# T5-bias attention and a maxout FFN in one kernel: transposes of q, k and x by DMA, and by TensorE

## The chip, the cores and the metric
The kernel runs on one core of one Trainium2 chip. The metric is device time in microseconds, the median of several runs.

## What is computed
Attention over 8 batches, 8 heads, 576 positions and 64 channels a head, with a T5 bias that depends on |i - j| alone, and after it an FFN that takes the largest of three products:

```python
scores = scale * np.matmul(q, k.transpose(0, 1, 3, 2))
scores = scores + bias.transpose(2, 0, 1)[None, :, :, :]   # bias_table[bucket(|i - j|)]
attn = np.exp(scores - scores.max(-1, keepdims=True)); attn = attn / attn.sum(-1, keepdims=True)
x = np.matmul(attn, v).transpose(0, 2, 1, 3).reshape(B * S, H * D)      # 4608 x 512
h = np.maximum(np.maximum(x @ w1, x @ w2), x @ w3)                      # 4608 x 768
out = h @ w_out                                                         # 4608 x 512
```
Inputs and output are float32; the kernel's matmuls work in bfloat16.

## The kernel before
**Visits.** The unit of work is a visit: one batch and one pair of heads, written (b, hp), 32 in all. Batch 0 has a prologue of its own (lines 1098 to 1195); batches 1 to 7 run through the main loop at line 1211. The 576 positions are four tiles of 128 and a rest of 64 (the tails, qtail and ktail, in which the rests of two heads stand on a diagonal). The 128 partitions of a pair hold 64 channels of one head and 64 of the other, so q and k are needed turned, channels on the partitions: qT[128, hp, 576] and kT[128, hp, 640].

**A visit.** TensorE makes scores into a score tile (pool ps_s, tag "sc": two tiles of two PSUM banks each, used in a ring also by the left keys, the left queries and batch 1's transposes). ScalarE takes the exponential into e4 (`scores` line 843, `key_scores` 854), VectorE multiplies the band near the diagonal by the exponential of the bias (`times_band` 803, `times_bandt` 906, `times_band_left` 918). One visit later `attend` (926) or `attend_rows` (976) multiplies by v, with a column of ones for the sums, and VectorE divides into x_sb (`quotients`). x_sb has positions on the partitions; the FFN wants xT, channels on the partitions.

**FFN.** It runs in chunks of 512 tokens beside the attention: chunk b-1 is spread over the visits (b, 2) to (b+1, 1), and what is left follows after the last visit. `ffn` (393) makes the parts: gates (two of the six blocks of 128 rows at a time, three products each, the largest of them), and outputs. `fill` (709) puts queued parts at given places of the plain visits; the tiled visits have them written out in a fixed order.

**Two forms of a tiled visit.** Before ROWS = (3, 0) a tiled visit uses `plain_gates` (492) and `attend` with single banks. From ROWS on ("rows") PSUM is shared out anew (`free_banks`, `banks(1)`, line 1220), all matmuls have 64 rows and run in pairs, one on each half of the array (`pair` 370, `gates` 518, `attend_rows`), and the third product of a visit's gates is made in the next visit (`thirds`). The order of one such visit is in `run` (557): FFN rows, the maximum of the visit before, `more_scores` (the fourth key score), bands, FFN rows, left queries, `ahead` (the first key score of the next visit), FFN rows.

**Transposes.** Batch 0's q, k and x are turned on TensorE into FFN banks (`first_transposes`, `more_transposes`, `x_transposes`). Batch 1's q and k are turned on TensorE into a score tile by `second_transposes` (781): all ten transposes, then VectorE copies q, ScalarE copies k. For batches 2 to 7 `transposes` (724) turns q and k by DMA transposes on SP's queue, ten a batch, at places listed in `places` (1198); x of batches 1 to 7 goes by DMA transposes at the end of the last quotients of a batch (969 and 1017).

**Order.** `inorder` keeps the order of the program on each engine, and all matmuls, transposes and copies named here are in order. The framework orders accesses to one PSUM tile by different engines; `other_banks` (128) lifts that between copies that read different banks. Loads stand on POOL's queue; `begin_qk` (206) begins the loads of a batch two ahead.

Of the kernel before, what the change touches and what calls it, by code (L numbers as in the profile page):

```python
# [39 lines left out]
def kernel(  # L40
# [12 lines left out]
    nc = tc.nc  # L53
# [3 lines left out]
    P = 128  # L57
# [3 lines left out]
    QS = 2 * P  # L61
    QM = 2 * QS
    KT = 4
    ROWS = (3, 0)
    DEEP = 6
    PACKETS = 6 * QM
    FCH = d_ff // P
# [32 lines left out]
    def free_banks():  # L100
        ps_f.release()
        ps_a.release()
# [9 lines left out]
    def tr(*args):  # L112
        inorder(nc.tensor.transpose(*args))
# [14 lines left out]
    def other_banks(later, earlier):  # L128

        for a in later:  # L130
            for b in earlier:
                tc.declare_no_dep(a.ins, b.ins, reason="they read different PSUM banks")
# [588 lines left out]
            hook()  # L721


    def transposes(b):

        made = qk_tiles()
        qk.append(made)

        def pair(g):
            for j in range(2):  # L730
                inorder(nc.sync.dma_start_transpose(  # L731
                    out=made[j][:, g, 0 : KT * P].rearrange("p (t n) -> p t n", t=KT),
                    in_=batch[b][j][:, g].rearrange("p t h d -> p (t h d)"),
                ))

        def left():
            for j, n in enumerate((S - KT * P, P)):
                inorder(nc.sync.dma_start_transpose(  # L738
                    out=made[j][:, :, KT * P : KT * P + n],
                    in_=(qtail, ktail)[j][b % 2][0:n].rearrange("p h c -> p (h c)"),  # L740
                ))

        return [lambda: pair(0), left] + [lambda g=g: pair(g) for g in range(1, HP)]

    def qk_tiles():
        return [qkt.tile([P, HP, n], BF16, tag=x, name=x) for x, n in (("qT", S), ("kT", (KT + 1) * P))]

# [30 lines left out]
        tr(tp[:, QS : QS + P], qtail[0][:, hp, :], ident[:])  # L778
        dve_copy(qk[0][0][:, hp, QS:], tp[:, 0 : S - QS])

    def second_transposes(made, hp):

        hs = slice(2 * hp, 2 * hp + 2)
        tp = ps_s.tile([P, 2, 2 * CH], BF16, tag="sc", name="tp")
        for j, tl in enumerate((qtail, ktail)):
            for t in range(KT):
                tr(tp[:, j, P * t : P * t + P], batch[1][j][:, t, hs, :].rearrange("p h d -> p (h d)"), ident[:])
            tr(tp[:, j, KT * P : KT * P + P], tl[1][:, hp, :], ident[:])
        main = [
            copy(  # L790
                made[j][:, hp, 0 : KT * P].rearrange("c (p t) -> c p t", t=KT),
                tp[:, j, 0 : KT * P].rearrange("c (t p) -> c p t", t=KT),
            )
            for j, copy in enumerate((dve_copy, act_copy))
        ]
        tail = [
            copy(made[j][:, hp, KT * P :], tp[:, j, KT * P : n])
            for j, (copy, n) in enumerate(((dve_copy, S), (act_copy, (KT + 1) * P)))
        ]
        other_banks([main[1], tail[1]], [main[0], tail[0]])  # L800
        other_banks([tail[0]], [main[1]])

    def times_band(hp, e4, t, lo, hi, put=lambda x: x):
        lo, hi = max(lo, P * t - P), min(hi, P * t + 2 * P)
# [121 lines left out]
    def attend(b, hp, e4, el, half):  # L926

        x = ps_a.tile([P, 6, AW], F32, tag="a", name="a")
        v, vl = vx[b % 2], vt[b % 2]
        for i in range(2):
            t = 2 * half + i
            c = slice(P * t, P * t + P)
            mm(
                x[:, 2 * i : 2 * i + 2, :], lhsT=el[:, c], rhs=vl[:, hp, :, 0:AW],
                start=True, stop=False, skip_group_check=True,
            )
            for par in range(2):  # L940
                for kt in range(KT):
                    mm(
                        x[:, 2 * i + par, :], lhsT=e4[:, kt, par, c], rhs=v[:, kt, 2 * hp + par, 0:AW],
                        start=False, stop=(kt == KT - 1), skip_group_check=True,
                    )
        n = 2 + half
        if half:
            mm(
                x[:, 4:6, :], lhsT=el[:, S - P : S], rhs=vl[:, hp, :, 0:AW],
                start=True, stop=False, skip_group_check=True,  # L950
            )
            for par in range(2):
                for kt in range(KT):
                    mm(
                        x[:, 4 + par, :], lhsT=el[:, S - 64 + P * kt + 64 * par :][:, 0:P],
                        rhs=v[:, kt, 2 * hp + par, 0:AW],
                        start=False, stop=(kt == KT - 1), skip_group_check=True,
                    )

        def quotients():  # L960
            rd = nrm.tile([P, 6], F32, tag="rd", name="rd")
            inorder(nc.vector.reciprocal(rd[:, 0 : 2 * n], x[:, 0 : 2 * n, D]))
            divided[b, hp, half] = inorder(nc.vector.tensor_tensor(
                out=x_sb[b][:, 2 * half : 2 * half + n, P * hp : P * hp + P].rearrange("p t (h d) -> p t h d", d=D),
                in0=x[:, 0 : 2 * n, 0:D].rearrange("p (t h) d -> p t h d", h=2),
                in1=rd[:, 0 : 2 * n].rearrange("p (t h) -> p t h", h=2).unsqueeze(3).to_broadcast([P, n, 2, D]),
                op=ALU.mult,
            ))
            if b and hp == HP - 1:
                for t in range(2 * half, 2 * half + 2 + half):  # L970
                    c = b * S + P * t
                    w = min(P, S - P * t)
                    inorder(nc.sync.dma_start_transpose(out=xT[:, :, c : c + w], in_=x_sb[b][P - w :, t, :]))
        return quotients

    def attend_rows(b, hp, e4, el):
# [28 lines left out]
        def end():  # L1005
            behind_rows(rows(True)[0], last)

            def quotients():
                n = KT + 1
                rd = nrm.tile([P, 2, n], F32, tag="rd", name="rd")  # L1010
                a = x[:, :, 0 : n * AW].rearrange("p h (t d) -> p h t d", d=AW)
                inorder(nc.vector.reciprocal(rd[:], a[:, :, :, D]))
                inorder(nc.vector.tensor_tensor(
                    out=x_sb[b][:, 0:n, P * hp : P * hp + P].rearrange("p t (h d) -> p h t d", d=D),
                    in0=a[:, :, :, 0:D], in1=rd[:].unsqueeze(3).to_broadcast([P, 2, n, D]), op=ALU.mult,
                ))
                if hp == HP - 1:
                    for t in range(n):
                        c = b * S + P * t
                        w = min(P, S - P * t)  # L1020
                        inorder(nc.sync.dma_start_transpose(out=xT[:, :, c : c + w], in_=x_sb[b][P - w :, t, :]))
            return quotients
        return end

# [107 lines left out]
    for hp in range(HP):  # L1132
# [42 lines left out]
        else:  # L1175
# [11 lines left out]
            if hp == 2:  # L1187
                x_transposes(2, 0)
                x_transposes(3, 0)
            else:  # L1190
                begin_qk(2)
                x_transposes(0, 1)
                fill(8, lambda: second_transposes(qk[1], 0))
            products(hp, el)
        late.append(lambda hp=hp, e4=e4, el=el: attend(0, hp, e4, el, 1))

    turns = {n: [] for n in range(2, B)}
    places = {2: ((1, 1, 0), (1, 1, 1), (1, 2, 0), (1, 3, 1), (2, 1, 0)), 3: ((2, 2, 0), (2, 2, 1), (2, 3, 0), (3, 0, 0), (3, 0, 1))}
    for n in range(4, B):
        places[n] = tuple((n - 1, hp, half) for hp, half in ((1, 0), (1, 1), (2, 0), (2, 1), (3, 0)))  # L1200

    def turn_ahead(*place):

        for n, order in places.items():
            if place == order[0]:
                turns[n] = transposes(n)
            if place in order:
                turns[n].pop(0)()

    turned = [lambda hp=hp: x_transposes(hp, 1) for hp in range(1, HP)]  # L1210
    for b, hp in [(b, hp) for b in range(1, B) for hp in range(HP)]:
# [5 lines left out]
        tiled = bool(stages)  # L1217
        rows = (b, hp) >= ROWS
        if (b, hp) == ROWS:
            free_banks()  # L1220
            ps_a, ps_f = banks(1)
            pending.clear()
            thirds = [after]
        rate = 8 if b == 1 or (b, hp) == (2, 0) else 13


# [13 lines left out]
            for c, tt in order[:2]:  # L1240
                scores(qT, kT, e4, c, tt)
        store_outputs()
        turn_ahead(b, hp, 0)
        early()
        if turned:
            turned.pop(0)()
# [19 lines left out]
        if rows:  # L1266
# [19 lines left out]
            def ahead():  # L1286
# [3 lines left out]
                    key_scores(*(x[:, n % HP, :] for x in qk[n // HP]), begun[0][0], 0)  # L1290

            run(
                lambda: key_scores(qT, kT, e4, 3), left, ahead, largest, bands, lambda: left_keys_rows(qT, kT, el)
            )
            thirds.append(after)
        elif tiled:
# [35 lines left out]

            visit(qT, kT, e4, order[2:], None if together else beside_scores, el=el if together else None)
        store_outputs()
        turn_ahead(b, hp, 1)
        early()
        if turned:
            turned.pop(0)()
        if not together:
            quotients = next_late()  # L1340
            times_band(hp, e4, 1, 0, QM, inorder)
            quotients()
        if b == 1 and hp + 1 < HP:
            second_transposes(qk[1], hp + 1)
        if hp == 1 and b > 1:
            pending.extend((n, [fn]) for n, fn in rest)
            rest.clear()
# [1 line left out]
        if hp == 1 and b + 1 < B:  # L1349
# [7 lines left out]
            if b == 1:  # L1357
                load_last_weights()
            load_pair(b + 1, 3)
        if hp == (2 if b == 1 else 1) and b + 2 < B:  # L1360
            begin_qk(b + 2)

        def queries():
# [24 lines left out]
    store_outputs()  # L1388
    for put in [next_late() for _ in late[:]]:
        put()  # L1390
    fill(13)
    store_outputs()
    for n in range(B - 1, NCH):
# [37 lines left out]
```

## Time and profile before
| | |
|---|---|
| median of 3 runs | 307.38 us (306.70 to 309.17) |
| the profiled execution | 306.96 us, its span 305.2 us |
| granted TensorE clock | 1.000 |
| ScalarE exponentials e<-sc, 128x1024 | 128 of 1026 ns |
| FFN matmuls psp<-xT,w_bf, 64x512 | 784 of 376 ns (latency of one; they overlap) |
| software queue q0 (loads) | 105664 packets, 95.5% of 16 engines' span |
| hardware queue q1 (stores and transposes) | 58304 packets, 41.6% |
| DMA transposes xT<-x_sb | 35, 5.6 us from issue to landing |
| DMA transposes qT<-q_sb and kT<-k_sb | 24 and 24, 5.8 and 5.6 us |
| DMA transposes of the tails | 6 and 6, 6.3 and 6.8 us |

The span is the time from the first to the last instruction of the core in one profiled execution; the execution's time has a little more around it. The share of busy time is a mean over stages with different limits, so stages are read by windows. A matmul's duration is its latency: matmuls follow each other faster than that, so the distance between starts tells their cost. "Idle before" and "waits" name what an engine waited for last.

### The profile page before, as it was taken

How to read it: one execution, taken by the hardware profiler on the slowest of the kernel's cores; microseconds unless marked ns; L12 is line 12 of the kernel's file. 1: busy time of each engine (PE TensorE's matmuls, PEld its weight loads, DVE VectorE, ACT ScalarE, POOL GpSimd, SP SyncE). 2: the span in 40 equal slices, each digit the busy share in tenths (PEclk: the TensorE clock that was granted, in tenths of full speed). 3: DMA queues.
4: the chain of work that ended last, by engine and by line, in shares of the span. 5: the costliest groups of instructions: out<-in, count | busy, mean ns of one | idle time of the engine just before them, and what ended most of it. 6: DMA issues, size and time to landing. Idle time of an engine off the chain costs nothing.

```text
span 305.2 us, 11001 instructions
## 1 busy us (share of the span) xinstructions
PE 295.5 (97%) x4745; PEld 183.7 (60%) x4745; DVE 206.3 (68%) x455; ACT 201.3 (66%) x270; POOL 143.7 (47%) x199
## 2 busy tenths in 40 slices
PE   8789999999999999999999999999999999999995
PEld 2367877765656676567666766676667654444442
DVE  6489888777776677676777677767776765453552
ACT  3999988977786787768776877677777720222211
POOL 8989677725839746774676469462000000000000
PEclk9999999999999999999999999999999999999999
DMA  9999999999999999999999999999623013202003
GB/s 160 187 203 194 176 137 120 114 165 128 223 150 121 150 131 205 174 143 192 181 139 135 202 162 146 138 197 171 79 46 140 6 40 94 84 0 108 31 0 137
DMA packets 165776, 40.51 MB, mean 133 GB/s; under 512 B 154584, under 2 KB 161248, under 8 KB 165728
## 3 DMA queue, kind: packets, MB, share of 16 engines
q0 software_dynamic: 105664, 16.66, 95.5%
q1 hardware_dynamic: 58304, 22.69, 41.6%
q8 instruction: 37, 0.61, 0.8%
q10 hardware_dynamic: 1760, 0.47, 0.7%
q14 instruction: 11, 0.09, 0.1%
HBM read 35.39 MB, written 9.45 MB: 147 GB/s over the span
## 4 chain that ended last, share of the span: by engine, by line
PE 80%; ACT 7%; DMA 6%; DVE 3%; SPq 2%; issue 1%; DVEq 0%; ACTq 0%
PE psp L109 32%; PE ps L109 15%; PE a L109 12%; PE sc L109 8%; PE pso L109 6%; ACT e L827 5%; DMA kT<-ktail 5%; PE sct L109 2%; PE warm L109 1%; PE scq L109 1%; ACT el L827 1%; SPq L738 1%; SPq L731 1%; DVE e L807 1%; DMA out_dram<-osb 1%
## 5 line engine op out<-in xcount | busy, mean ns | idle before, releaser
L827 ACT ACTIVATE e<-sc 128x1024 bf16<-128x1024 f32 x128 | 129.0, 1026 | 29.3 <-PE sc L109 28.0
L109 PEld LDWEIGHTS <-w_bf 64*128 64x128 bf16 (+1 forms) x1112 | 75.8, 95 | 55.3 <-issue 1.9
L109 PE MATMUL psp<-xT,w_bf 64*128 64x512 bf16 x784 | 97.2, 376 | 0.0
L807 DVE TENSOR_TENSOR e<-e,hank 128x512 bf16<-128x512 bf16 (+2 forms) x120 | 56.1, 473 | 13.9 <-ACT e L827 13.2
L109 PE MATMUL ps<-xT,w_bf 128*128 128x512 bf16 (+1 forms) x328 | 59.1, 332 | 0.0
L109 PE MATMUL sc<-qT,kT 64*128 64x256 bf16 (+1 forms) x352 | 48.5, 319 | 2.3 <-ACT e L827 1.1
L109 PEld LDWEIGHTS <-kT 64*128 64x128 bf16 (+1 forms) x712 | 30.0, 94 | 24.8 <-issue 6.8
L109 PE MATMUL a<-vx,e 64*128 64x65 bf16 (+1 forms) x1664 | 44.9, 190 | 0.0
L199 POOL DMA_DIRECT2D k_sb<-in_k_dram x48 | 36.2, 764 | 17.8 <-DMA vx<-in_v_dram 7.8
L199 POOL DMA_DIRECT2D q_sb<-in_q_dram x48 | 36.4, 767 | 15.1 <-DMA vx<-in_v_dram 5.7
L109 PEld LDWEIGHTS <-e 64*128 64x128 bf16 (+1 forms) x1664 | 40.8, 95 | 4.3
L109 PEld LDWEIGHTS <-hT 64*128 64x128 bf16 (+1 forms) x462 | 28.3, 95 | 18.7 <-DVE hT L551 1.6
L167 POOL DMA_DIRECT2D vx<-in_v_dram x28 | 24.8, 893 | 19.5 <-PE a L109 5.4
L109 PE MATMUL psp<-wo_bf,hT 64*128 64x256 bf16 (+1 forms) x360 | 31.7, 305 | 0.0
L421 ACT ACTIVATE m<-ps 128x512 bf16<-128x512 f32 x14 | 8.4, 597 | 34.3 <-PE ps L109 34.3
L827 ACT ACTIVATE el<-sct 128x576 bf16<-128x576 f32 (+2 forms) x36 | 21.7, 605 | 14.0 <-PE sct L109 13.9
L109 PEld LDWEIGHTS <-el 64*128 64x128 bf16 (+1 forms) x676 | 26.4, 94 | 7.0 <-issue 4.4
L109 PE MATMUL a<-vt,el 64*128 64x65 bf16 (+1 forms) x260 | 29.5, 198 | 0.2 <-DVE m L511 0.2
L551 DVE TENSOR_TENSOR hT<-psp,m 128x1024 bf16<-128x1024 f32 (+1 forms) x20 | 18.7, 956 | 9.1 <-PE psp L109 9.1
L109 PE MATMUL pso<-wo_bf,hT 128*128 128x512 bf16 (+2 forms) x102 | 21.7, 366 | 0.0
L430 DVE TENSOR_TENSOR m<-ps,m 128x512 bf16<-128x512 f32 x14 | 9.7, 692 | 17.0 <-PE ps L109 17.0
L537 DVE TENSOR_TENSOR m<-psp,m 128x1024 bf16<-128x1024 f32 x15 | 18.4, 1225 | 3.3 <-PE psp L109 3.1
(82 smaller groups left out, 292.8 us busy)
## 6 DMA issues: line engine op xcount, KB each, us to landing
out_dram<-osb SPq DMA_DIRECT2D x35, 256.0 KB, 4.7
vx<-in_v_dram POOLq DMA_DIRECT2D x28, 128.0 KB, 6.7
q_sb<-in_q_dram POOLq DMA_DIRECT2D x50, 64.0 KB, 5.3
k_sb<-in_k_dram POOLq DMA_DIRECT2D x48, 64.0 KB, 5.3
w_bf<-in_moe_w_dram POOLq DMA_DIRECT2D x2, 512.0 KB, 8.5
xT<-in_k_dram SPq DMA_DIRECT2D x6, 128.0 KB, 4.5
hank<-w_dr SPq DMA_DIRECT2D x2, 384.0 KB, 5.7
w_bf<-in_moe_w_dram POOLq DMA_DIRECT2D x1, 768.0 KB, 8.1
```

What stands on the lines that cost most here:

```text
L109: made = inorder(nc.tensor.matmul(*args, **kw))
L167: in_turn(b, nc.gpsimd.dma_start(out=dst[:, t, h0:h1, :], in_=x[:, t, h0:h1, :]), P * (h1 - h0))
L199: in_turn(b, nc.gpsimd.dma_start(out=dst[:, g, :, par, :], in_=part), KT * P)
L421: nc.scalar.activation(out=st[fb]["m0"][:], in_=ps0, func=ACTF.Copy)
L430: inorder(nc.vector.tensor_tensor(out=m[:], in0=ps1, in1=st[fb]["m0"][:], op=ALU.max))
L537: return lambda: inorder(nc.vector.tensor_tensor(out=m[0][:], in0=ps1(), in1=m[0][:], op=ALU.max,))
L551: inorder(nc.vector.tensor_tensor(out=out_[:, i : i + n], in0=ps2()[:, i : i + n], in1=m[0][:, i : i + n], op=ALU.max,))
L731: inorder(nc.sync.dma_start_transpose(out=made[j][:, g, 0 : KT * P].rearrange("p (t n) -> p t n", t=KT), in_=batch[b][j][:, g].rearrange(" ...
L738: inorder(nc.sync.dma_start_transpose(out=made[j][:, :, KT * P : KT * P + n], in_=(qtail, ktail)[j][b % 2][0:n].rearrange("p h c -> p (h c)"),
L807: put(nc.vector.tensor_tensor(out=e4[:, t, :, lo:hi], in0=e4[:, t, :, lo:hi], in1=hank[:, 2 * hp : 2 * hp + 2, c0:c1][:, :, ::-1], op=ALU. ...
L827: made = nc.scalar.activation(out=out_, in_=in_, func=ACTF.Exp, scale=inv_sqrt_d)
```

## The change
All of q, k and x, for every batch, are turned on TensorE. One new function, `turn(n)`, replaces `second_transposes`, `transposes`, `turn_ahead` and the DMA transposes of x: it takes a score tile of two banks, turns q into the first and k into the second for visit n+1, has them copied, then turns x of visit n-1 into the free columns of both banks (384 columns in the first, 192 in the second) and has them copied. Batches from 2 on have q and k loaded in pairs, so one copy each does. The plain visits call it after their scores, the rows visits ahead of the fourth key score, and once more it is called after the last visit. ROWS moves from (3, 0) to (2, 2), the first tiled visit: no tiled visit is plain any more, the first one has no third product from before, and the queued parts of the FFN are emptied ahead of it. `begin_qk(b + 2)` is called after visit (b, 2) for all b; it was after (b, 1) for b above 1.

```diff
-    ROWS = (3, 0)
+    ROWS = (2, 2)
...
-    def transposes(b):
-        made = qk_tiles()
-        qk.append(made)
-        def pair(g):
-            for j in range(2):
-                inorder(nc.sync.dma_start_transpose(
-                    out=made[j][:, g, 0 : KT * P].rearrange("p (t n) -> p t n", t=KT),
-                    in_=batch[b][j][:, g].rearrange("p t h d -> p (t h d)"),
-                ))
...
-    def second_transposes(made, hp):
...
+    def turn(n):
+
         tp = ps_s.tile([P, 2, 2 * CH], BF16, tag="sc", name="tp")
...
+        L = (KT + 1) * P
+        by_bank = [], []
+
+        def put(bank, dst, src):
+            made = (dve_copy, act_copy)[bank](dst, src)
+            other_banks([made], by_bank[1 - bank])
+            by_bank[bank].append(made)
+
+        b, hp = divmod(n + 1, HP)
+        if b < B:
+            if len(qk) == b:
+                qk.append(qk_tiles())
+            for j, tl in enumerate((qtail, ktail)):
+                for t in range(KT):
+                    part = batch[b][j][:, hp, t] if b > 1 else batch[b][j][:, t, 2 * hp : 2 * hp + 2]
+                    tr(tp[:, j, P * t : P * t + P], part.rearrange("p h d -> p (h d)"), ident[:])
+                tr(tp[:, j, KT * P : L], tl[b % 2][:, hp, :], ident[:])
+            for j, n_cols in enumerate((S, L)):
+                dst, src = qk[b][j][:, hp, 0:n_cols], tp[:, j, 0:n_cols]
+                if b == 1:
+                    put(
+                        j, dst[:, 0 : KT * P].rearrange("c (p t) -> c p t", t=KT),
+                        src[:, 0 : KT * P].rearrange("c (t p) -> c p t", t=KT),
+                    )
+                    dst, src = dst[:, KT * P :], src[:, KT * P :]
+                put(j, dst, src)
+        b, hp = divmod(n - 1, HP)
+        if b > 0:
+            for j, places in enumerate((((0, 0), (1, P), (2, 2 * P)), ((KT, 64), (KT - 1, 0)))):
+                for t, c in places:
+                    tr(tp[:, j, L + c : L + c + P], x_sb[b][:, t, P * hp : P * hp + P], ident[:])
+            w = 3 * P
+            put(0, xT[:, hp, b * S : b * S + w], tp[:, 0, L : L + w])
+            put(1, xT[:, hp, b * S + w : b * S + S], tp[:, 1, L : L + S - w])
...
-            if b and hp == HP - 1:
-                for t in range(2 * half, 2 * half + 2 + half):
-                    c = b * S + P * t
-                    w = min(P, S - P * t)
-                    inorder(nc.sync.dma_start_transpose(out=xT[:, :, c : c + w], in_=x_sb[b][P - w :, t, :]))
...
-                fill(8, lambda: second_transposes(qk[1], 0))
+                fill(8, lambda: turn(HP - 1))
...
         if (b, hp) == ROWS:
+            while pending:
+                fill(13)
             free_banks()
             ps_a, ps_f = banks(1)
             pending.clear()
-            thirds = [after]
+            thirds = [lambda: (lambda: None, lambda parts=1: lambda: None)]
...
-        turn_ahead(b, hp, 0)
...
             run(
-                lambda: key_scores(qT, kT, e4, 3), left, ahead, largest, bands, lambda: left_keys_rows(qT, kT, el)
+                lambda: (turn(HP * b + hp), key_scores(qT, kT, e4, 3)), left, ahead, largest, bands,
+                lambda: left_keys_rows(qT, kT, el),
             )
...
-        if b == 1 and hp + 1 < HP:
-            second_transposes(qk[1], hp + 1)
+        if not rows:
+            turn(HP * b + hp)
...
-        if hp == (2 if b == 1 else 1) and b + 2 < B:
+        if hp == 2 and b + 2 < B:
             begin_qk(b + 2)
...
         put()
+    turn(HP * B)
     fill(13)
```

More of the change, by code (lines that the diff above doesn't have):

```diff
@@ L721, in fill @@
             hook()
-    def transposes(b):
-        made = qk_tiles()
-        qk.append(made)
-        def pair(g):
-            for j in range(2):
-                inorder(nc.sync.dma_start_transpose(
-                    out=made[j][:, g, 0 : KT * P].rearrange("p (t n) -> p t n", t=KT),
-                    in_=batch[b][j][:, g].rearrange("p t h d -> p (t h d)"),
-                ))
[L736 to L743, printed above, removed]
     def qk_tiles():
@@ L779, in more_transposes @@
         dve_copy(qk[0][0][:, hp, QS:], tp[:, 0 : S - QS])
-    def second_transposes(made, hp):
-        hs = slice(2 * hp, 2 * hp + 2)
+    def turn(n):
         tp = ps_s.tile([P, 2, 2 * CH], BF16, tag="sc", name="tp")
[L785 to L801, printed above, removed]
+        L = (KT + 1) * P
[30 more added lines that the diff above has]
+            put(1, xT[:, hp, b * S + w : b * S + S], tp[:, 1, L : L + S - w])
@@ L1016, in quotients @@
                 ))
[L1017 to L1021, printed above, removed]
             return quotients
@@ L1192 @@
                 x_transposes(0, 1)
-                fill(8, lambda: second_transposes(qk[1], 0))
+                fill(8, lambda: turn(HP - 1))
             products(hp, el)
         late.append(lambda hp=hp, e4=e4, el=el: attend(0, hp, e4, el, 1))
[L1197 to L1208, printed above, removed]
     turned = [lambda hp=hp: x_transposes(hp, 1) for hp in range(1, HP)]
@@ L1334 @@
         store_outputs()
-        turn_ahead(b, hp, 1)
         early()
```

## The prediction, made before the changed kernel was run
> **What bounds the kernel now.** I read the page first (busy times, clock, chain), then the windows stage by stage, then the waits of TensorE, then the timeline of two places: one steady visit, and the one turn of a head pair that TensorE already makes in batch 1. A visit is one pass of the main loop, written (batch, head pair).
>
> ```profile
> PE 295.5 (97%) x4745; PEld 183.7 (60%) x4745; DVE 206.3 (68%) x455; ACT 201.3 (66%) x270; POOL 143.7 (47%) x199
> ```
> ```profile
> core 0: us, PE busy (x) PEld busy (x) DVE busy (x) ACT busy (x) POOL busy (x), PEclk, DMA share, GB/s
> 45.70:52.41 6.71, 6.40 (x107) 5.10 (x107) 5.66 (x17) 6.01 (x10) 5.33 (x7) 1.00 2.46 118
> 52.41:58.19 5.78, 5.78 (x97) 4.55 (x97) 4.30 (x13) 5.19 (x9) 2.98 (x4) 1.00 1.98 139
> 172.66:203.97 31.31, 31.31 (x659) 20.65 (x656) 22.18 (x43) 23.60 (x28) 20.43 (x29) 1.00 2.01 166
> ```
> The last line is four visits of one batch, 7.8 us each: TensorE is busy for all of it at full clock (PEclk 1.00), VectorE and ScalarE for about 22 to 24 us of 31.31. Busy alone is not proof, so I check it by columns: in one gate visit the chain has 48 half-height matmuls of 512 columns in pairs (0.86 us per 8, so 5.2 us), 90 half-height attention matmuls (0.75 + 0.63 us), four scores (0.22 us each), left keys twice 0.12 and left queries 0.12: 7.8 us. Nothing is idle there. What is put on TensorE in this stage is paid in full; what is taken off the DMA queues is paid back only where TensorE waited for a DMA. The chain of waits seems to show such places, the list of TensorE's waits denies them:
>
> ```profile
> 82.17 8.31 DMA kT<-ktail
> ...
> 115.26 6.87 DMA kT<-ktail
> ```
> ```profile
> PEld L109 <- DMA kT<-ktail: 0.8, 2, 0.5
> ```
> The chain walks back through a transfer's whole flight, though TensorE worked under it. It sat idle for that transfer 0.8 us, in two places. That is the whole DMA time to be won on TensorE.
>
> **What is removed.** 95 DMA transposes (24 + 24 of q and k, 6 + 6 of the tails, 35 of x), about 1.2 us of SP's queue each, and their packets. SP holds only the stores besides, and nothing on the path waits for those. Gain: at most the 0.8 us above.
>
> **What is added, in pieces.** Turn n transposes q and k of visit n+1 (10 matmuls) and x of visit n-1 (5). q and k are new for the 24 visits of batches 2 to 7, x for the 28 of batches 1 to 7: 240 + 140 = 380 matmuls, and 104 more copies out of PSUM. The turn in batch 1 shows the price of one:
>
> ```profile
> 50.50 0.39 PE L113 MATMUL tp<-ident,q_sb 128*128 128x128 bf16 x4
> ...
> 51.00 0.22 PE L113 MATMUL tp<-ident,ktail 128*128 128x128 bf16 x1
> 51.01 0.81 PEld L109 LDWEIGHTS <-w_bf 128*128 128x128 bf16 x8
> 51.06 1.04 PE L109 MATMUL ps<-xT,w_bf 128*128 128x256 bf16 x8
> ...
> 51.63 0.78 DVE L126 COPY qT<-tp 128x512 bf16<-128x512 bf16 x2
> 51.72 0.80 ACT L123 ACTIVATE kT<-tp 128x512 bf16<-128x512 bf16 x2
> ...
> 52.41 0.61 PE L109 MATMUL sc<-qT,kT 64*128 64x256 bf16 x8 [0.31 <-DVE qT L126]
> ```
> Ten transposes take 50.50 to 51.06, 0.056 us each. Then TensorE goes on at once with FFN matmuls while the copies run, and at the end it waits 0.31 us for them. Visit (1,2), with this turn, takes 6.71 us; (1,3), with the same 24 FFN matmuls and no turn, 5.78.
>
> The new turn differs in its order, and this is where most of my number comes from. TensorE issues q's and k's transposes, VectorE is told to copy q (bank 0) and ScalarE k (bank 1), and only then TensorE issues x's five transposes, into the free columns of the same two banks. No matmul of other work stands between. The code lifts the order only between copies of different banks (other_banks); between a copy out of a bank and the next matmul into it the order stays. So TensorE stops until both copies are over, and behind it stand the next scores, the rest of the FFN pair, and through them ScalarE's next exponentials.
>
> [...]
>
> **Rows visits, (2,2) to (7,2): 21 turns of 15.** The turn stands between the FFN rows and the fourth key score, at 187.86 in this visit:
>
> ```profile
> 186.74 1.02 ACT L827 ACTIVATE e<-sc 128x1024 bf16<-128x1024 f32 x1
> 187.21 1.23 DVE L551 TENSOR_TENSOR hT<-psp,m 128x1024 bf16<-128x1024 f32 x1 [0.60 <-PE psp L109]
> ...
> 187.86 0.39 PE L109 MATMUL sc<-qT,kT 64*128 64x512 bf16 x2
> ...
> 188.29 1.03 ACT L827 ACTIVATE e<-sc 128x1024 bf16<-128x1024 f32 x1 [0.53 <-PE sc L109]
> ```
> From there: 0.10 us to change from half-height to full matmuls (the gap at 245.74 to 245.85, before the full-height attention), 0.50 to the start of the last k transpose, 0.25 until ScalarE starts (a transpose ends 0.22 after its start, ScalarE starts 0.03 behind a matmul), 0.72 for the copy of 128x640 (0.453 at 320 columns and about 0.88 ns for each more, from the el rows 0.597 at 512 and 0.653 at 576), 0.03 back, 0.11 to 0.28 for the x transposes (two if those of bank 0 ran earlier, five if not), 0.10 back to half height: 1.8 to 2.0, I take 1.9. ScalarE is free at 187.76 and its exponential was due only at 188.29; VectorE ends its maximum at 188.44 and copies q (about 0.45, rows 0.42 at 512 and 0.48 at 640) before k is out. x's copies (0.35 each) hide while TensorE makes the score. ScalarE then has 5.9 + 1.1 us a visit of 9.7, VectorE 5.5 + 0.8: neither becomes the bound. 21 x 1.9 = 39.9.
>
> **Early visits.** TensorE waits as above, but ScalarE's copy stands behind its exponentials. (1,1): ten transposes were there, the copies end at 45.07 and 16 FFN matmuls that hid them now come after: +1.5. (1,2): the same, copies end at 52.52: +1.4. (1,3) and (2,0): ten new ones from 57.22 and 63.21; ScalarE ends its second exponential at 58.56 and 64.55, then copies k: +2.3 each. (2,1): no attention stands between the scores and the turn, so the score tile itself is free only when the first exponential ends (70.0), k is copied after the second (70.97 + 0.71): from 68.80 to 72.0, +3.2. Together 10.7.
>
> **The ends.** (7,3) turns only x: 5 x 0.056 and two changes of height, 0.5. The last turn waits for VectorE's last quotients (they end at 248.42; FFN now starts at 247.35) and adds 0.28: 1.4.
>
> **Row pairs from (2,2).** Windows: (2,2) takes 7.79 us with 22 FFN units of 512 columns, (2,3) 8.14 with 24, (3,0) 8.1 to 8.4 with 24; a rows visit takes 7.8 with 24. Emptying the pending list takes the same matmuls, and the change of banks (about 0.6 us lost at (3,0)) moves with it. Gain 0.8, between 0 and 1.5.
>
> **Moved.** The 11 loads of begin_qk (0.65 to 0.77 us of POOL's queue each, about 8 us) come one visit later and are wanted by the turn of (b+1, 3), five visits on, over 40 us: hidden by that lead, costing their landing time (5.3 us) if it were gone.
>
> **Sum.** 39.9 + 10.7 + 0.5 + 1.4 - 0.8 = 51.7; I leave the 0.8 us of DMA waits out. The profiled execution took 306.96 us (span 305.2 and 1.8 around it), 0.4 under the median of 307.38. 306.96 + 51.7 = 358.7, say 359.
>
> **Rivals.**
> *No wait.* x's transposes run beside the copies: 380 x 0.056 = 21.3, 22 changes of height there and back 4.4, the end's wait 1.1, (2,1)'s tile 1.2, less 0.8: +27.2, 334. For it: the turn in batch 1 ran on beside its copies. Against: there it ran on into other banks. 10 in 100.
> *Longer wait.* ScalarE or VectorE is late at the turn: if the copy of k stands behind more work for 0.6 us in each of 21 turns, +12.6, 372. For it: every early visit behaves so. Against: in the steady visit ScalarE has idled 0.53 us at this point. 14 in 100.
> *Not slower.* The chain's pieces are real waits: DMA 6% and SP's queue 2% of the span, 24.4 us, vanish, and the turns cost only their 21.3: 304. It decides once the idle time that DMAs end on TensorE exceeds the turns' price; the waits give 0.8 us. 2 in 100.
>
> **How the numbers follow.** The main sum (345 to 366) has 64 in 100; 10 lie between it and the no-wait case, where part of the wait is covered. The range goes from the no-wait case to the longer wait, 334 to 372; outside lie the gain, half of the no-wait case and half of the longer one, some 15 in 100. About 1% is what a measurement of this kernel can tell from no change. Faster by over 1%: 0.02. Within 1%: 0.02, a sum in which all but 3 us is hidden. Slower: 0.96.
>
> **What would show it.** Right: in a steady batch four visits take 38 to 39 us in place of 31.3; in each turn TensorE has an idle piece of 0.8 to 1.1 us before the x transposes, ended by the copy of k on ScalarE; TensorE's busy share falls; the granted clock stays 1.00. Wrong: five x transposes directly behind the k ones, visits of about 8.9 us; or the idle piece ended by VectorE; or a clock below 1.00 from the added idle time (the windows here stay at 1.00 even where TensorE is idle a tenth of the time); or an early stage that absorbs its 10.7 us in waits that it had already.

## The result, and the profile after

The changed kernel takes 361.23 us (median of 4 runs, 360.4 to 361.6) where the kernel before took 307.04 us beside it (4 runs, 306.62 to 309.17): a ratio of 1.1745, 95% interval 1.1685 to 1.1805. The forecast was 359, range 334 to 372. The profiled execution took 361.6 us, its span 359.6.

The page of the changed kernel, busy times, clock and the two DMA queues:

```profile
PE 323.9 (90%) x5203; PEld 202.8 (56%) x5211; DVE 226.5 (63%) x500; ACT 226.0 (63%) x320; POOL 143.6 (40%) x199
...
PEclk9999999999999999999999999999999999999999
...
q0 software_dynamic: 105664, 16.66, 62.9%
q1 hardware_dynamic: 9952, 11.08, 9.0%
...
PE 81%; ACT 12%; DVE 3%; issue 1%; DMA 1%; ACTq 0%; DVEq 0%
```

TensorE's busy time rose by 28.4 us, the span by 54.4: the other half is idle time, so its share fell from 97% to 90%. The DMA queues were relieved as intended (q0 from 95.5% to 62.9% of the span, q1 from 41.6% to 9.0%), and loads land sooner (q in 3.2 us instead of 5.3). None of that shortens the path. The last line, the chain of waits, now has 12% of ScalarE in it.

TensorE's waits, first those of its matmuls, then two of those of its weight loads (microseconds in total, times, longest):

```profile
PE tp L113 <- ACT kT L123: 22.5, 26, 1.3
...
PE tp L113 <- ACT e L822: 1.2, 1, 1.2
PE tp L113 <- DVE x_sb L958: 0.7, 2, 0.4
```
```profile
PEld L113 <- DVE qT L126: 20.6, 26, 1.4
...
PEld L113 <- DMA q_sb<-in_q_dram: 1.3, 3, 0.4
```

The first line is the new wait: 26 times the transposes stop for ScalarE's copy of k. 26 turns make q, k and x together (those of (1,1) to (7,2)), so every one of them does. The weight loads' line is the same stop seen on the other half of TensorE (the load of x waits for VectorE's copy of q, which ends earlier); the two are not added.

Now stage by stage. Windows cut at the first score of (1,0), (1,1), (1,2), (1,3), (2,0), (2,1), (2,2) and at the end of the attention, before and after; the columns are start:end, its length, then each engine's busy time with its number of instructions (PE, PEld, DVE, ACT, POOL), TensorE's clock, the DMA engines' share and GB/s:

```profile
31.62:38.77 7.15, 7.15 (x123) 5.86 (x122) 6.23 (x18) 6.69 (x12) 3.92 (x7) 1.00 1.94 176
38.77:45.70 6.93, 6.84 (x110) 5.40 (x110) 5.81 (x17) 5.96 (x11) 5.69 (x9) 1.00 1.51 130
...
58.19:64.18 5.99, 5.95 (x96) 4.54 (x96) 4.55 (x13) 5.56 (x9) 4.55 (x7) 1.00 1.07 122
64.18:71.50 7.32, 7.27 (x90) 4.02 (x89) 5.39 (x15) 5.47 (x8) 1.49 (x2) 1.00 1.91 133
71.50:247.35 175.85, 175.00 (x3546) 113.83 (x3546) 124.08 (x243) 130.40 (x156) 90.35 (x121) 1.00 1.67 144
247.35:305.20 57.85, 54.08 (x260) 24.59 (x256) 27.88 (x42) 10.43 (x18) 0.00 (x0) 1.00 0.20 65
```
```profile
33.24:40.38 7.14, 7.14 (x121) 5.85 (x121) 6.15 (x18) 6.68 (x12) 5.33 (x8) 1.00 1.78 175
40.38:48.86 8.48, 7.28 (x115) 5.76 (x115) 6.35 (x18) 6.30 (x12) 6.92 (x10) 1.00 1.48 100
48.86:56.98 8.12, 6.77 (x112) 5.46 (x112) 6.34 (x19) 6.45 (x11) 6.59 (x10) 1.00 1.46 92
56.98:65.04 8.06, 6.78 (x113) 5.46 (x112) 5.28 (x16) 6.39 (x10) 4.09 (x6) 1.00 1.42 144
65.04:73.09 8.05, 6.76 (x111) 5.45 (x111) 5.27 (x16) 6.39 (x10) 8.05 (x12) 1.00 1.14 75
73.09:84.50 11.41, 9.29 (x109) 5.54 (x112) 6.88 (x19) 6.01 (x9) 8.40 (x12) 1.00 1.64 143
84.50:300.60 216.10, 198.57 (x3946) 128.49 (x3945) 138.83 (x277) 151.40 (x197) 74.70 (x100) 1.00 0.60 62
300.60:359.60 59.00, 54.44 (x260) 24.87 (x261) 28.22 (x43) 10.76 (x19) 0.00 (x0) 1.00 0.14 54
```

In the tiled visits, (2,2) to the end of the attention, 175.85 us became 216.10. TensorE was idle 0.85 us there before and is idle 17.5 now, while it is busy 23.6 longer. The rest is in the early visits: they were full to within a few tenths and now have 1.2 to 2.1 us of idle time each.

One steady visit of the changed kernel, the timeline around its turn (start, length, engine and operation; in brackets the idle time before it and what ended it):

```profile
215.72 1.02 ACT L822 ACTIVATE e<-sc 128x1024 bf16<-128x1024 f32 x1
...
216.96 0.40 PE L113 MATMUL tp<-ident,q_sb 128*128 128x128 bf16 x4
...
217.47 0.22 PE L113 MATMUL tp<-ident,ktail 128*128 128x128 bf16 x1
217.72 0.70 ACT L123 ACTIVATE kT<-tp 128x640 bf16<-128x640 bf16 x1 [0.98 <-PE tp L113]
217.72 0.46 DVE L126 COPY qT<-tp 128x576 bf16<-128x576 bf16 x1 [0.30 <-PE tp L113]
...
218.48 0.44 PE L113 MATMUL tp<-ident,x_sb 128*128 128x128 bf16 x5 [0.79 <-ACT kT L123]
...
218.85 0.39 PE L109 MATMUL sc<-qT,kT 64*128 64x512 bf16 x2
...
219.28 1.02 ACT L822 ACTIVATE e<-sc 128x1024 bf16<-128x1024 f32 x1
```

The reader sees the whole cost in one place. From the first transpose to the score that stood behind the turn, TensorE spends 1.89 us, and its matmuls account for only some 1.1 of it. ScalarE had been idle 0.98 us when k came, copied at once, and all five x transposes, the three into the bank of q too, started 0.06 us after that copy had ended. VectorE's copy of q out of that bank was over at 218.18, so the order that holds them goes by the whole tile `tp` and not by the bank: `other_banks` frees the copies from each other, but not the transposes. The turns of this stage start at 177.65, 187.43, 197.26, 207.16 and 216.96: 9.83 us a visit, against 31.31 / 4 = 7.83 before, so 2.00 us a turn.

### The profile page after: what moved, and what is told of

Read it like the earlier page. It is cut to its first block, busy times and chain, and to the rows that moved or that the text cites. A ratio compares the mean times of both kernels' runs of the same rounds, so it can differ in the third digit from the quotient of the medians.

```text
span 359.6 us, 11855 instructions
## 1 busy us (share of the span) xinstructions
PE 323.9 (90%) x5203; PEld 202.8 (56%) x5211; DVE 226.5 (63%) x500; ACT 226.0 (63%) x320; POOL 143.6 (40%) x199
## 3 DMA queue, kind: packets, MB, share of 16 engines
q0 software_dynamic: 105664, 16.66, 62.9%
## 4 chain that ended last, share of the span: by engine, by line
PE 81%; ACT 12%; DVE 3%; issue 1%; DMA 1%; ACTq 0%; DVEq 0%
PE psp L109 31%; PE ps L109 14%; PE a L109 11%; PE tp L113 8%; PE sc L109 8%; ACT e L822 5%; ACT kT L123 5%; PE pso L109 5%; PE sct L109 2%; ACT el L822 1%; PE warm L109 1%; PE scq L109 1%; DVE e L802 1%; DVE x_sb L958 1%; DMA out_dram<-osb 1%
## 5 line engine op out<-in xcount | busy, mean ns | idle before, releaser
L109 PEld LDWEIGHTS <-w_bf 64*128 64x128 bf16 (+1 forms) x1120 | 74.6, 95 | 55.8 <-issue 1.2
L109 PE MATMUL psp<-xT,w_bf 64*128 64x512 bf16 x800 | 98.8, 376 | 0.6 <-DVE x_sb L1003 0.6
L802 DVE TENSOR_TENSOR e<-e,hank 128x512 bf16<-128x512 bf16 (+2 forms) x120 | 57.6, 485 | 12.5 <-ACT e L822 12.1
L109 PE MATMUL ps<-xT,w_bf 128*128 128x512 bf16 (+1 forms) x317 | 56.9, 331 | 0.2
L109 PE MATMUL sc<-qT,kT 64*128 64x512 bf16 (+1 forms) x336 | 48.1, 328 | 2.1 <-ACT e L822 1.3
L109 PEld LDWEIGHTS <-kT 64*128 64x128 bf16 (+1 forms) x700 | 28.6, 94 | 23.5 <-issue 6.3
L113 PE MATMUL tp<-ident,x_sb 128*128 128x128 bf16 x140 | 12.5, 218 | 23.2 <-ACT kT L123 22.5
L123 ACT ACTIVATE kT<-tp 128x640 bf16<-128x640 bf16 (+2 forms) x32 | 20.1, 647 | 18.8 <-PE tp L113 18.8
L126 DVE COPY qT<-tp 128x576 bf16<-128x576 bf16 (+4 forms) x39 | 16.2, 424 | 18.6 <-PE tp L113 18.6
L113 PEld LDWEIGHTS <-x_sb 128*128 128x128 bf16 x160 | 11.1, 96 | 28.6 <-DVE qT L126 20.6
```

The costliest lines, as they stand in the source:

```text
L109: made = inorder(nc.tensor.matmul(*args, **kw))
L123: return inorder(nc.scalar.activation(out=out_, in_=in_, func=ACTF.Copy))
L126: return inorder(nc.vector.tensor_copy(out_, in_))
L802: put(nc.vector.tensor_tensor(out=e4[:, t, :, lo:hi], in0=e4[:, t, :, lo:hi], in1=hank[:, 2 * hp : 2 * hp + 2, c0:c1][:, :, ::-1], op=ALU. ...
```

## The experiments

Two theories stood against each other. *Mine*: half of the cost is matmul time and the other half is TensorE waiting between its transposes of k and of x until the copy of k is over. *The first rival*: the matmuls and their changes of height cost it all, and the idle time is only put down to the copy. Further questions were what q and k, x, and the row pairs each bring, and whether the relief of the DMA queues is worth anything.

**All transposes ahead of all copies.** The same work in another order: no matmul into a bank that is being read.

```diff
         b, hp = divmod(n + 1, HP)
+        xb, xh = divmod(n - 1, HP)
...
+        if xb > 0:
+            for j, places in enumerate((((0, 0), (1, P), (2, 2 * P)), ((KT, 64), (KT - 1, 0)))):
+                for t, c in places:
+                    tr(tp[:, j, L + c : L + c + P], x_sb[xb][:, t, P * xh : P * xh + P], ident[:])
+        if b < B:
             for j, n_cols in enumerate((S, L)):
...
         if b > 0:
-            for j, places in enumerate((((0, 0), (1, P), (2, 2 * P)), ((KT, 64), (KT - 1, 0)))):
-                for t, c in places:
-                    tr(tp[:, j, L + c : L + c + P], x_sb[b][:, t, P * hp : P * hp + P], ident[:])
```

> All fifteen transposes of a turn ahead of all its copies; the same matmuls and copies. Theory (TensorE stops for the copies between k and x): the 22.5 us that TensorE waited for k's copy in 26 turns go, and little comes back, since the score and 16 FFN matmuls (1.95 us) now cover the copies (about 1.3 us from the last k transpose): 339 us, between 335 and 343. Rival 1 (the wait only moves to the next user of the tile or of k): 355 or more. Rival 2 (the transposes cost by their number and the changes of array height, the wait was cover for other work): 358 to 362.

Measured: 338.53 us (4 runs, 338.16 to 340.96) beside 306.49 for the kernel before, ratio 1.1039 (1.0976 to 1.1101). One steady turn of it, in the timeline:

```profile
203.14 0.40 PE L113 MATMUL tp<-ident,q_sb 128*128 128x128 bf16 x4
...
203.65 0.22 PE L113 MATMUL tp<-ident,ktail 128*128 128x128 bf16 x1
...
203.71 0.44 PE L113 MATMUL tp<-ident,x_sb 128*128 128x128 bf16 x5
204.08 0.39 PE L109 MATMUL sc<-qT,kT 64*128 64x512 bf16 x2
204.19 0.70 ACT L123 ACTIVATE kT<-tp 128x640 bf16<-128x640 bf16 x1 [1.26 <-PE tp L113]
```

The same matmuls now take 0.94 us (203.14 to 204.08) in place of 1.89, and the copy of k runs under the score. Four visits take 35.97 us (176.00 to 211.97), 1.16 us a turn over before. The wait for k's copy is gone from the list of waits. The ratio fell by 0.0706, 21.7 us, and the stretch from the first score of batch 1 to the first FFN matmul behind the last turn from 268.66 us (33.24 to 301.90) to 246.91 (34.51 to 281.42), 21.75: the 22.5 us of that line but for what other waits took back. My theory stands, and its rival falls: the wait is real and not a label. In this order no matmul writes a bank of `tp` that is being read: both copies start at 204.19, behind the last transpose. No kernel here tried such a write, nor transposes that wait for the copy of their own bank alone.

**The copy of k made twice**, in the 24 turns that make q and k of batches 2 to 7: a longer copy and nothing else on TensorE.

```diff
-                put(j, dst, src)
+                for _ in range(1 + j * (b > 1)):
+                    put(j, dst, src)
```

> ScalarE copies k twice into the same place in the 24 turns of batches 2 to 7. Theory (the wait for k's copy is on the path): 24 x 0.70 = 16.9 us more, 378 us. Rival (ScalarE has about two us idle in a visit, so a copy there is free): 361 to 363.

Measured: 381.55 us (379.98 to 382.39), ratio 1.2417 (1.2352 to 1.2481). The page and the waits:

```profile
PEclk9999998888999999999999999999999999999999
```
```profile
PE tp L113 <- ACT kT L123: 40.1, 26, 2.0
```

The wait grew from 22.5 to 40.1 us, 17.6 / 24 = 0.73 us a copy, so each turn waits for this copy to its end. The expected 378 was 3.6 us short. In four slices the granted clock is below full (8 in the clock row, mean 0.987), which the changed kernel does not show: the trace has it at 0.50 in three stretches of 3.4 us, from 64.2, 74.5 and 84.7 (eight attention matmuls of 128x65 take 0.64 us at 65.37, 0.41 at 69.80). The four runs separate this: 379.98 us at a mean clock of 0.995, 380.92 at 0.991, 382.17 and 382.39 at 0.987, so about 1.2 us for each 0.004. An estimate from them for the full clock is 378.5 to 379, and most of the remainder is the clock.

**Only q and k on TensorE, x by DMA as before**, and **only x on TensorE, q and k of batches 2 to 7 by DMA as before**. Both keep row pairs from (2,2).

```diff
...
-        if b > 0:
+        if False:
...
+                        inorder(nc.sync.dma_start_transpose(out=xT[:, :, c : c + w], in_=x_sb[b][P - w :, t, :]))
```
```diff
...
-        if b < B:
+        if b < 2:
...
+        turn_ahead(b, hp, 0)
...
```

> q and k turned on TensorE as in the changed kernel, x by DMA transposes as before. Theory: no matmul into a bank being read, so no wait: 21 turns of ten x 0.056 and two changes of height (0.76) = 16, early turns about 4, row pairs -0.8: 326 us. Rival (54 us spread over 380 transposes, 0.14 each): 240 x 0.14 = 34, 341 us.

> x turned on TensorE as in the changed kernel, q and k of batches 2 to 7 by DMA transposes as before. Theory: 22 turns of five x 0.056 and two changes of height (0.48) = 10.6, early visits about 3, end 1.2, row pairs -0.8: 321 us. Together with the run that has only q and k on TensorE the two parts then cost about 33 us, and the missing 21 of the whole change's 54 are the wait that only both together have. Rival (cost by number of transposes): 140 x 0.14 = 20, 327 us, and the two parts add up to 54.

Measured: q and k alone 326.52 us (ratio 1.0636, 1.0586 to 1.0686), x alone 325.82 us (1.0625, 1.0556 to 1.0694). The steady visit, by the distance between starts of transposes over four visits, in a table of all versions:

| version | us a visit | over before |
|---|---|---|
| before | 7.83 | |
| x alone | 8.31 | 0.48 |
| q and k alone | 8.64 | 0.81 |
| all, transposes ahead of copies | 8.99 | 1.16 |
| the change | 9.83 | 2.00 |
| the change, k copied twice | 10.56 | 2.73 |

Each part alone costs about its matmuls; together, in the order of the change, they cost 0.71 us a turn more than the two added up (0.48 + 0.81), and 0.84 more than with the transposes ahead. The two parts add up to 20.0 + 19.3 = 39.3 us over before, and the change costs 54.2: 14.9 us are missing, as much as 21 turns of 0.71, where 21 us were expected. The rival had the parts add up to 54.

The 326.52 was expected. The x part was 5 us above its 321: its steady visits are right (0.48 expected and found), the early ones are not. (1,3) and (2,0) take 7.19 us there in place of 5.78 and 5.99. (2,1) costs 1.3 us more beside the six output matmuls emptied into it. The timeline of x alone at the end of (2,0) shows what I had left out:

```profile
68.27 0.56 DVE L979 TENSOR_TENSOR x_sb<-a,rd 128x384 bf16<-128x384 f32 x1
...
68.88 0.34 PE L113 MATMUL tp<-ident,x_sb 128*128 128x128 bf16 x3 [0.96 <-DVE x_sb L979]
```

In a plain visit the turn follows directly on VectorE's last quotients, and the second half of x is not there yet. In the whole change this second wait lies under the wait for k's copy and costs nothing more.

**Only the row pairs**, on the kernel before.

```diff
-    ROWS = (3, 0)
+    ROWS = (2, 2)
...
+            while pending:
+                fill(13)
...
```

> The kernel before with ROWS = (2, 2), all transposes as before. Theory: 0.8 us less (0 to 1.5), 306 beside 306.5 to 307, too little to tell by the time; the profile should show visits (2,2) to (3,0) together about 0.8 shorter. Rival (the row pairs carry part of the loss, since the pending FFN parts are emptied with nothing beside them): 1 to 3 us more.

Measured: 311.26 us (12 runs, 309.14 to 314.01) beside 307.75 (17 runs), ratio 1.0099 (1.0064 to 1.0135). My expectation fell: not 0.8 us faster but some 3 slower. Its trace has pieces of idle time on TensorE that end with nothing the profile shows, a line that the matmul waits of the kernel before do not have:

```profile
PE psp L109 <- issue: 2.4, 3, 1.2
```

The four longest of the attention, in the timeline of the weight loads:

```profile
94.03 0.54 PEld L109 LDWEIGHTS <-w_bf 64*128 64x128 bf16 x7 [0.88 <-issue]
...
119.48 1.19 PEld L109 LDWEIGHTS <-w_bf 64*128 64x128 bf16 x14 [0.73 <-issue]
125.50 0.52 PEld L109 LDWEIGHTS <-w_bf 64*128 64x128 bf16 x6 [1.61 <-issue]
...
151.25 1.41 PEld L109 LDWEIGHTS <-w_bf 64*128 64x128 bf16 x15 [1.19 <-issue]
```

The matmuls, which run on while weight loads pause, stand idle 0.58, 0.43, 1.22 and 0.69 us there, 2.9 together, about what the kernel lost. Counted by TensorE's recorded instructions (matmuls, weight loads and waits on semaphores), the four lie at numbers 2753, 3777, 4033 and 5057, and the distances (1024, 256, 1024; 509, 128 and 509 of them weight loads) are all multiples of 256. The table of queues has one of kind "instruction" (packets, MB, share), 16 KB a packet:

```profile
q8 instruction: 38, 0.62, 0.9%
```

TensorE's 9711 recorded instructions are 37.9 times 256, beside 38 packets; in the change 10477 (5203 matmuls, 5211 weight loads, 63 others) are 40.9 times 256, beside 41. So I formed the theory that TensorE's instructions come by this queue, 256 to a packet, and that some packets come late because the DMA engines are full (q0 94.0%, q1 40.7%). Both parts are inferences from these counts; no trace shows an instruction waiting for a packet. To test it I lightened the load: the same kernel and the kernel before, both with the queued output stores dropped.

```diff
     def store_outputs():
-        while stores:
-            stores.pop(0)()
+        stores.clear()
```

> The row pairs alone again, but with nearly all output stores of the loop left out (the queued stores are dropped, so most of the output is never written). Theory: the row pairs alone were some 3 us slower than before because TensorE's instructions arrived late at four places where the DMA engines were full; with a lighter load the four idle pieces go, and the time falls from 311.3 to 306 to 308. Rival: the idle pieces come from the row pairs themselves (their order of matmuls), or from the loads alone: 310 to 312, and the pieces stay where they were.

> The kernel before with the same output stores left out: the control for the run above. The trace of before has no such idle pieces and nothing on the path waits for a store, so both theories expect no change: 306 to 308. If it falls clearly below 306, the stores cost time in the kernel before as well, and the run above shows less.

Measured on one chip: row pairs without stores 306.97 us (12 runs, 306.35 to 308.82; ratio 0.9979, 0.9950 to 1.0009), before without stores 306.22 (12 runs, 305.79 to 307.40; 0.9955, 0.9929 to 0.9982), before 307.19. By the ratios the stores cost the kernel before 0.45%, 1.4 us (1.0 between the medians), and the row pairs 1.2%, 3.7 us. The weight loads of row pairs, with and then without stores:

```profile
PEld L109 <- issue: 19.3, 63, 1.6
```
```profile
PEld L109 <- issue: 15.7, 62, 0.8
```

The list of the kernel before has 15.6 us in 63 pieces, 0.8 the longest. So the extra 3.7 us of pieces go when the stores go (the longest one left in the tiled visits is 0.72, with 0.60 of the matmuls): the order of the matmuls alone does not make them. Nor do the stores alone, since the kernel before has them and none of the pieces. That the late thing is a packet of instructions is not shown. What the other traces add is the place: the piece of 0.60 us lies at number 6337, and one of 0.37 us in the kernel before without stores at 5825, both, like the four, 193 beyond a multiple of 256. What is left of the row pairs, 306.97 against 306.22, lies within the two intervals: no gain is seen, a loss of 0.75 us is possible.

**The change without its row pairs**, pairs from (3,0) as before.

> The whole change with row pairs from (3, 0) as before, not from (2, 2). Theory: inside the whole change the DMA queues are not full (63% and 9%), so TensorE's instructions are not late and the row pairs bring their 0.8 us: without them 361.5 to 363. Rival: the row pairs cost the 3 us that they cost alone: 357.5 to 359.

Measured: 361.39 us (8 runs, 360.7 to 364.44), ratio 1.1719 (1.1664 to 1.1774); the change has 1.1745 (1.1685 to 1.1805). The 3 us that row pairs cost alone are not lost here, which fits the lighter queues. A gain of 0.8 is within the intervals, so the whole times leave it open. The profiled executions, one of each, show one: from the first score of (2,2) to the first FFN matmul behind the last turn the kernel without row pairs takes 219.65 us (83.75 to 303.40), the change 217.40 (84.50 to 301.90) and 1.3 for six output matmuls that it has emptied ahead, so 0.95 less. The clock is 1.00 in both stretches.

**The DMA transposes issued twice**, into the same place, in the kernel before, to see what their load is worth: x alone, then q, k and x.

```diff
-    inorder(nc.sync.dma_start_transpose(out=xT[:, :, c : c + w], in_=x_sb[b][P - w :, t, :]))
+    for _ in range(2):
+        inorder(nc.sync.dma_start_transpose(out=xT[:, :, c : c + w], in_=x_sb[b][P - w :, t, :]))
...
```

> The kernel before with each of the 35 DMA transposes of x issued twice, into the same place. Theory (DMA transposes lie beside TensorE's work, SP's queue has room: 95 x 1.2 = 114 us of some 250): no change, within 1%, 305 to 309. Rival (they cost what the chain of waits gives them, 6% DMA and 2% of SP's queue for 95): a third of 24 us more, about 315.

> The kernel before with all 95 DMA transposes issued twice. Theory: in a batch 30 transposes of 1.2 us or more stand on SP's queue, some 38 us, where a batch takes 31.3: the queue falls behind and q and k come late, 6 x 7 = 40 us more, 345. Rival (the cover is wider: a later transpose still comes in time, since each batch is turned a batch ahead and the queue catches up): 307 to 315.

Measured: 372.03 us (ratio 1.2080, 1.2011 to 1.2148) and 463.42 (1.5059, 1.4986 to 1.5131). Both theories missed by far, because the experiment measures another thing. The waits of x twice, first SP's queue, then TensorE's:

```profile
SPq L1023 <- DMA xT<-x_sb: 61.8, 25, 4.8
```
```profile
PE psp L109 <- DMA xT<-x_sb: 31.7, 4, 15.0
PE sc L109 <- DMA kT<-k_sb: 12.7, 4, 5.3
```

The second transpose into one place waits on SP's queue until the first has landed, 25 times for 2.5 us on average, and all that is queued behind comes late. That says what a stalled SP queue costs, and nothing on the load of the DMA engines. These two are inconclusive for their question.

## Why the prediction was right, step by step

**The wait.** The step that carried the number was that TensorE stops between k and x until both copies are over. It is shown three times: by the line of 22.5 us, by its going with the order (-21.7 us), and by its growing with the copy (0.73 us a copy).

**Its pieces.** Predicted and measured in the steady turn: 0.50 and 0.51 to the last k transpose (216.96 to 217.47), 0.25 and 0.25 to ScalarE's start, 0.72 and 0.70 for the copy, 0.03 and 0.06 back, and five transposes, not two, behind it: the 0.11 to 0.28 was at its upper end. So 2.00 us and not 1.9, and 21 turns give 2.1 us more than the sum had.

**Early visits.** Predicted +1.5, +1.4, +2.3, +2.3 and +3.2; measured +1.55, +1.41, +2.28, +2.06 and +4.09. Of the last, 1.3 us are six output matmuls of 0.216 us that stood in (2,2) before and are now emptied ahead of it, so 2.8 against 3.2. That makes 10.1 us where the sum had 10.7.

**The ends.** The part after the attention grew by 1.15 us against 1.4 for the last turn.

**Row pairs.** The windows of the stage fit a gain: 40.25 + 1.3 for the six matmuls is 41.55, where 21 turns and the 0.5 of (7,3) make 42.5. So does the profile of the change without them, 0.95 us longer there. The whole times can't confirm it: inside the change no difference is measured, and on the kernel before the row pairs show no gain even without the stores. The 0.8 was read from windows of neighbouring visits with different work, and its bounds should have reached below nothing: alone the row pairs cost some 3 us by a way that no window of before shows.

**DMA.** "A gain of at most 0.8 us" held: the transposes left, q1 fell to 9.0%, and no stage became shorter. The kernel before pays about 1 us for its stores (307.19 against 306.22), which its profile does not show (spans of 305.2 and 305.1), so something of the 0.8 may be gained and can't be seen beside the 54 us.

**Not in the sum.** The first score of batch 1 starts 1.6 us later, though nothing of the change lies before it. Three of VectorE's multiplies by the band, at 20.08, 21.45 and 22.49, ran slower there, by 0.63, 0.35 and 0.63 us. GpSimd copied beside the later two; the first was over before that copy began, so why it was slow isn't shown. Two of the three, before and after:

```profile
20.07 0.28 DVE L807 TENSOR_TENSOR e<-e,hank 128x256 bf16<-128x256 bf16 x1
21.50 0.28 DVE L807 TENSOR_TENSOR e<-e,hank 128x256 bf16<-128x256 bf16 x1
```
```profile
20.08 0.91 DVE L802 TENSOR_TENSOR e<-e,hank 128x256 bf16<-128x256 bf16 x1
21.13 2.13 POOL L356 COPY bandt<-hank 64x768 bf16<-64x768 bf16 x2
22.49 0.91 DVE L802 TENSOR_TENSOR e<-e,hank 128x256 bf16<-128x256 bf16 x1
```

It isn't the change's doing: the same start lies at 31.7 to 32.1 us in other versions with `turn` and at 34.5 in one, where the clock stood at 0.50 from 23.9 to 27.3 (four scores at 25.15 take 0.61 us, at 20.34 0.39). So a profiled execution carries 1.5 us or more of chance in its prologue. Together: turns and row pairs +1.95 (41.55 for 39.9 + 0.5 - 0.8), early visits -0.6, the end -0.25, the prologue +1.6, so 51.7 + 2.7 = 54.4, the difference of the spans. The sum came close by the wait and its pieces; the prologue's part is chance.

**The rivals.** *No wait*, 334: not the change, but the kernel with transposes ahead of copies is nearly this case, at 338.5. *Longer wait*, 372: in every steady turn ScalarE stood idle (0.98 us) when k came. *Not slower*, 304: excluded by the queues, which were relieved without effect.

## What to carry to other kernels

Where TensorE fills a tile of PSUM, has it copied out and then writes into the same tile again, and the program keeps that order, the copy lies on TensorE's path, even if the second write goes to free columns, and here even where it goes to the other bank of the tile: 0.8 us a turn, 22.5 in all, and moving the five transposes ahead of the copies gives nearly all of it back. With TensorE busy 97% of the span before, work taken off the DMA queues onto it cost more than its 15 transposes of 0.056 us (1.16 us a turn in the best order tried); no version here that writes the whole output beats the kernel before. Before crediting a relief of the DMA queues, read TensorE's own list of waits, not the chain: the chain counted 24.4 us and the list 0.8.

## What the runs showed of the hardware that was not expected

Unnamed idle pieces ("issue") stop TensorE's matmuls for 0.4 to 1.2 us (its weight loads for 0.7 to 1.6) at four places of the kernel with only the row pairs, where q0 stands at 94.0% and q1 at 40.7%. With the stores left out (q0 93.3%, q1 34.9%) one of 0.60 us is left, and the kernel before without stores has one of 0.37. All six lie 193 beyond a multiple of 256 in the order of TensorE's recorded instructions. The kernel before, at 95.5% and 41.6%, has none over 0.6 us of its weight loads in its tiled visits, so a full queue alone does not bring them about; what else has to meet it stays open.

The granted clock, 1.00 in the change with TensorE busy 90% of the span, fell to a mean of 0.987 with k copied twice (86%), 0.935 with x transposed twice (84%) and 0.874 with all transposed twice (71%). Five of the stretches at 0.50, each of about 3.4 us, can be set against the 3.4 us ahead of them. With k copied twice TensorE was busy 1.38, 1.38 and 1.40 us there (ahead of 64.2, 74.5 and 84.7). With the transposes ahead of the copies it was busy 1.59 us (20.48 to 23.89). In the change without row pairs it was busy 1.39 us (76.00 to 79.41), the longest pause 1.22 us. The change has as little in the same visit (1.38 of 3.40, 77.3 to 80.7) and kept its clock, so the idle time alone does not decide it; what else does is not shown. The waits of the steady turns brought no such stretch: with k copied twice the three make up the whole loss of the mean clock.
